# A fused attention and token-MLP kernel: a replanned order of score groups, first loads on two queues, a half-size weight load, and filler matmuls

**Chip, cores, metric.** One core of one Trainium2 chip. The metric is the time of one execution in device microseconds (us). The profile's span is 1.8 us shorter than the time of the same execution.

## The reference, cut to what matters

```python
q, k, v: (8 batches, 12 heads, 448, 64)
scores = (q @ k.T) / 8 - log(448);  x = sigmoid(scores) @ v      # heads side by side: (8, 448, 768)
wq, wk = x @ w_q, x @ w_k                                        # both (8, 448, 64)
mixed  = ((wq @ wk.T) / 8) @ x
out    = relu(mixed) @ w_out
```

## The kernel before

The work is cut into 24 *pairs* (two batches by two heads), each with seven score groups. A string, PLAN, gives the order of TensorE's groups: `S` scores of one group (then a sigmoid on ScalarE), `P` values, `q`/`k` the transposes of one pair's q or k, `x` transposes of the attention output, `W N U M m O` the MLP. Loads and casts follow in a fixed ORDER. Every load passes one queue; GpSimd (Pool) casts it to bf16; TensorE takes everything in the plan's order.

```python
    p_ld = pool("ld", 3)            # load buffers of each of q, k, v
    p_qk = pool("qk", 8)            # transposed q, k
    def scores(n, i):
        ...                                             # 4 matmuls 64x64, k stationary
        nc.scalar.activation(at, sc[:, :, 0:S], ACTF.Sigmoid, bias=bias_t, scale=attn_scale)
    def load_weights():             # w_q and w_k, each for both halves of the partitions
        for b2 in range(2):
            for x, w in enumerate((moe_w_q, moe_w_k)):
                o = 64 * (x ^ b2)
                nc.sync.dma_start(out=wqk32[HALF[b2], :, o : o + 64], in_=w.rearrange("(h d) n -> d h n", d=HD))
    def pump_loads():               # the next load in ORDER, if its buffer's last owner has been cast
        ...
                if n >= 3 and (nm, n - 3) not in cast:
                    break
    def pump():                     # the next cast in ORDER, on Pool
        ...
                    nc.gpsimd.tensor_copy(out=wqk16, in_=wqk32)     # the weights, in their turn
        ...
                cast1(n, nm, nc.gpsimd)
    nc.sync.dma_start(out=q0, in_=src["q"])
    nc.sync.dma_start(out=k0[:, :, cols(KA)], in_=src["k"][:, :, cols(KA)])
    nc.sync.dma_start(out=k0[:, :, cols(KB)], in_=src["k"][:, :, cols(KB)])
    ...                             # cut: 32 matmuls on zeros, then
    tr_part("q", q016, IA, "v")
    tr_part("q", q016, IB, "s")
    tr_part("k", k016, KA, "v", free2[-1])
```

## Time and profile before

| | before |
|---|---|
| time, median of the first 4 runs | 210.30 us (210.11 to 210.66) |
| span of the profiled execution | 209.4 us (this execution took 211.18) |
| first sigmoid | 6.47 us |
| 64th sigmoid (first of pair 9) | 68.33 us |
| from there to the last output chunk | 135.64 us |

The two times at the bottom are starts of single instructions in the trace.

### The profile page before, as it was taken

To read this page: it belongs to the slowest core of one execution; us is meant where nothing else is said; L and a number is where in the kernel's file an instruction comes from. 1 tells how busy PE (TensorE), PEld (TensorE's weight loads), DVE (VectorE), ACT (ScalarE), POOL (GpSimd) and SP (SyncE) were. 2 spreads that over 40 slices of the span, in tenths; PEclk is the share of its full clock that TensorE was granted. 3 is DMA by queue.
4 is the path that set the end of the run, shared out by engine and by line. 5 is a ranking of instruction groups with operands and counts; after the bars stand their busy time and mean duration, and the time that the engine had idled before them with its cause. 6 is when DMAs were issued, how large, how long until landed. Compare 5 with 4: busy or idle time off the path is not lost.

```text
span 209.4 us, 6320 instructions
## 1 busy us (share of the span) xinstructions
PE 197.0 (94%) x2630; PEld 117.5 (56%) x2630; DVE 121.9 (58%) x208; ACT 170.8 (82%) x193; POOL 72.6 (35%) x85
## 2 busy tenths in 40 slices
PE   8498988889999999999999999999999999999991
PEld 7254544556546656656656565655565555655561
DVE  2135555755598746664889675645788654554321
ACT  3689999979999999999998989889898998055220
POOL 2477755577877842730022700251110000000000
PEclk9759999999999999999999999999999999999999
DMA  5999999999999999997065463355203252154785
GB/s 174 374 381 380 381 173 290 381 384 384 383 384 383 379 381 385 399 389 253 5 199 130 145 181 79 78 147 195 51 29 78 75 152 70 27 134 104 200 203 174
DMA packets 28684, 47.59 MB, mean 227 GB/s; under 512 B 5360, under 2 KB 24432, under 8 KB 28656
## 3 DMA queue, kind: packets, MB, share of 16 engines
q1 hardware_dynamic: 27616, 45.03, 67.1%
q10 hardware_dynamic: 1040, 2.16, 2.7%
q8 instruction: 20, 0.33, 0.7%
q14 instruction: 8, 0.07, 0.1%
HBM read 36.18 MB, written 11.01 MB: 225 GB/s over the span
## 4 chain that ended last, share of the span: by engine, by line
PE 75%; DMA 16%; POOL 2%; SPq 1%; ACT 1%; issue 1%; DVE 1%; DVEq 0%; ACTq 0%; POOLq 0%
PE po L283 27%; PE sc L154 15%; PE pv L173 13%; DMA v<-in_v_dram 9%; DMA k<-in_k_dram 8%; PE px L191 5%; PE pw L215 3%; PE ptq L131 3%; PE ptk L131 3%; PE pt L240 3%; PE pm L264 2%; ACT at L159 1%; POOL k L118 1%; POOL v L118 1%; SPq L107 1%; PE pk L227 1%
## 5 line engine op out<-in xcount | busy, mean ns | idle before, releaser
L159 ACT ACTIVATE at<-sc,bias_t 128x896 bf16<-128x896 f32 x168 | 155.4, 1020 | 12.6 <-PE sc L154 11.7
L283 PE MATMUL po<-wout,mx 128*128 128x384 bf16 (+1 forms) x342 | 60.6, 324 | 0.0
L154 PE MATMUL sc<-qt,kt 64*64 64x448 bf16 x672 | 57.7, 367 | 2.5 <-ACT at L159 1.8
L283 PEld LDWEIGHTS <-mx 128*128 128x128 bf16 x342 | 30.9, 98 | 24.3 <-issue 7.0
L173 PE MATMUL pv<-at,v 64*64 64x448 bf16 x672 | 41.8, 352 | 1.1 <-POOL v L118 1.1
L178 DVE CAST xt<-pv 128x896 bf16<-128x896 f32 x24 | 26.2, 1091 | 23.4 <-PE pv L173 23.4
L308 DVE COPY o<-po 128x384 f32<-128x384 f32 x45 | 25.1, 557 | 24.7 <-PE po L283 24.4
L154 PEld LDWEIGHTS <-kt 64*64 64x64 bf16 x672 | 21.9, 105 | 23.7 <-issue 12.6
L118 POOL CAST q<-q 128x896 bf16<-128x896 f32 x23 | 21.5, 933 | 33.3 <-issue 26.3
L118 POOL CAST v<-v 128x896 bf16<-128x896 f32 x24 | 22.3, 934 | 22.6 <-PE pv L173 18.0
L118 POOL CAST k<-k 128x896 bf16<-128x896 f32 x23 | 21.5, 933 | 19.4 <-PE ptk L131 15.7
L173 PEld LDWEIGHTS <-v 64*64 64x64 bf16 x672 | 20.5, 107 | 11.2 <-POOL v L118 1.4
L138 DVE COPY kt<-ptk 128x896 bf16<-128x896 bf16 x23 | 14.3, 620 | 10.3 <-PE ptk L131 10.2
L196 DVE COPY xn<-px 128x512 bf16<-128x512 bf16 x48 | 18.0, 417 | 2.9 <-PE px L191 2.9
L306 ACT COPY o<-po 128x384 f32<-128x384 f32 x10 | 4.8, 478 | 15.7 <-PE po L283 15.7
L256 DVE TENSOR_SCALAR mx<-pm 128x896 bf16<-128x896 f32 x15 | 16.3, 1088 | 1.8 <-PE pm L264 1.4
L138 DVE COPY qt<-ptq 128x896 bf16<-128x896 bf16 x23 | 14.1, 619 | 4.5 <-PE ptq L131 3.7
L131 PE MATMUL ptq<-ident,q 128*128 128x128 bf16 x161 | 13.7, 228 | 1.4 <-POOL q L118 1.4
L191 PE MATMUL px<-ident,xt 128*128 128x128 bf16 x192 | 14.7, 220 | 0.2 <-DVE o L308 0.2
L191 PEld LDWEIGHTS <-xt 128*128 128x128 bf16 x192 | 11.6, 98 | 4.6 <-issue 3.8
L131 PE MATMUL ptk<-ident,k 128*128 128x128 bf16 x161 | 13.3, 224 | 0.6 <-POOL k L118 0.6
L131 PEld LDWEIGHTS <-q 128*128 128x128 bf16 x161 | 9.9, 102 | 6.7 <-issue 3.7
(43 smaller groups left out, 93.8 us busy)
## 6 DMA issues: line engine op xcount, KB each, us to landing
q<-in_q_dram SPq DMA_DIRECT2D x24, 448.0 KB, 8.0
v<-in_v_dram SPq DMA_DIRECT2D x24, 448.0 KB, 7.5
k<-in_k_dram SPq DMA_DIRECT2D x23, 448.0 KB, 7.8
out_dram<-o SPq DMA_DIRECT2D x44, 192.0 KB, 3.0
w<-in_moe_w_out_dram SPq DMA_DIRECT2D x6, 384.0 KB, 5.8
out_dram<-o ACTq DMA_DIRECT2D x10, 192.0 KB, 3.2
wqk<-in_moe_w_q_dram SPq DMA_DIRECT2D x2, 192.0 KB, 9.4
wqk<-in_moe_w_k_dram SPq DMA_DIRECT2D x2, 192.0 KB, 8.5
```

The source lines that it names most:

```text
L118: eng.tensor_copy(out=t16.rearrange("p i b d -> p b i d"), in_=ld.pop((nm, n)).rearrange("p b (i d) -> p b i d", i=NI),)
L131: nc.tensor.transpose(ps[:, i].rearrange("p h n -> p (h n)"), t16[:, i].rearrange("p b d -> p (b d)"), ident16,)
L138: nc.vector.tensor_copy(out=t[:, hs], in_=ps[:, :, hs, :].rearrange("p i h n -> p h i n"))
L154: nc.tensor.matmul(sc[HALF[h], b2, 0:S], qk["k", n][HALF[b2], h, i, :], qk["q", n][HALF[b2], h].rearrange("p i n -> p (i n)"), start=True, ...
L159: nc.scalar.activation(at, sc[:, :, 0:S], ACTF.Sigmoid, bias=bias_t, scale=attn_scale)
L173: nc.tensor.matmul(ps[HALF[b2], h, 0:S], ld["v16", n][HALF[h], i, b2, :], ats[n, i][HALF[h], b2, :], start=(i == 0), stop=(i == NI - 1),)
L178: nc.vector.tensor_copy(out=xts[j][:, :, 0:S], in_=ps[:, :, 0:S])
L191: nc.tensor.transpose(ps[:, m, h].rearrange("p b d -> p (b d)"), xts[j][:, h, m * P : (m + 1) * P], ident16,)
L196: nc.vector.tensor_copy(out=xns[u][:, :, b2, 2 * HD * j : 2 * HD * (j + 1)].rearrange("p m (h d) -> p m h d", h=2), in_=ps[:, :, :, b2, :],)
L256: nc.vector.tensor_scalar(dst, ps, moe_scale, 0.0, ALU.mult, ALU.max)
L283: nc.tensor.matmul(ps, mxs[u][c].rearrange("p b s -> p (b s)")[:, m * P : (m + 1) * P], wout16[:, c, w0:w1], start=(c == 0), stop=(c == NC ...
L308: nc.vector.tensor_copy(out=o[:, nb * NB : (nb + 1) * NB], in_=ps)
```

## The change

Intent: keep ScalarE from running dry in the first 45 us by a better order, bring the first q and k in sooner, and keep the clock of TensorE up.

```diff
-    p_qk = pool("qk", 8)
+    p_qk = pool("qk", 14)
@@ weights: half the bytes, other half copied on chip
-        for b2 in range(2):
-            for x, w in enumerate((moe_w_q, moe_w_k)):
-                o = 64 * (x ^ b2)
-                nc.sync.dma_start(
-                    out=wqk32[HALF[b2], :, o : o + 64], in_=w.rearrange("(h d) n -> d h n", d=HD)
-                )
+        for x, w in enumerate((moe_w_q, moe_w_k)):
+            nc.sync.dma_start(
+                out=wqk32[:, :, 64 * x : 64 * x + 64], in_=w.rearrange("(h d) n -> d h n", d=HD)
+            )
+    def cast_weights():
+        nc.gpsimd.tensor_copy(out=wqk16[HALF[0]], in_=wqk32)
+        nc.gpsimd.dma_start(out=wqk16[HALF[1]], in_=wqk16[HALF[0]])
@@ start
-    nc.sync.dma_start(out=q0, in_=src["q"])
-    nc.sync.dma_start(out=k0[:, :, cols(KA)], in_=src["k"][:, :, cols(KA)])
-    nc.sync.dma_start(out=k0[:, :, cols(KB)], in_=src["k"][:, :, cols(KB)])
+    for t32, nm in ((q0, "q"), (k0, "k")):
+        for b2, eng in ((0, nc.sync), (1, nc.scalar)):
+            eng.dma_start(out=t32[:, b2], in_=src[nm][:, b2])
...
-    for _ in range(32):
-        nc.tensor.matmul(ps[:, 0, 0:P], zeros, zeros, start=True, stop=True)
+    keep_warm(28)
...
     tr_part("q", q016, IB, "s")
+    keep_warm(9)
     tr_part("k", k016, KA, "v", free2[-1])
+    keep_warm(5)
@@ ORDER is now made from the plan: a load stands where its first use stands; weights 6 places before W
+    places = [(first["W"] - 6, 0)] + [(first["O"] - 14 + 2 * c, c) for c in range(1, 7)]
@@ PLAN, rows of pairs 0 to 6 of 24 (D is a filler of two 64x448 matmuls)
-        "SSSKqSSSSkq",
-        "SPPPPPSkSSPkSPqSS",
-        "SxPqSPPPPSPPSqSPPSkPSPP",
-        "SxPSSPkSSSkPPSkP",
-        "SPPPPSqSqSSqxSxSk",
-        "SSqkPPSPPPPSPqSkSSxPPPP",
-        "SPPPSkqSWWWSWWWWSWWWWSWSx",
+        "SSSKPDDDSkSqSPkSPPD",
+        "SPDDSkSPDDSPqSqSSxq",
+        "SPPkSqSPPPPSkSPqSPSPP",
+        "SPPPSPkSkSSSqSx",
+        "SqxPSPqSPkSPPPSPqSqSPPP",
+        "SPPPPSqSxSkSSkxPPSPPP",
+        "SkPSPkSqSWWWSkWSWWWSWWWW",
... (17 rows cut)
```

`keep_warm(n)` issues n matmuls of 128 columns on zeros. Not shown: in `W` the output half is `x ^ b2`, to fit the copied weights.

More of the change, by code (lines that the diff above doesn't have):

```diff
@@ L84 @@
     wqk16 = singles.tile([P, H, P], BF16, name="wqk16")
-    wqk32 = singles.tile([P, H, P], F32, name="wqk32")
+    wqk32 = singles.tile([NP, H, P], F32, name="wqk32")
     ident = singles.tile([P, P], F32)
@@ L215, in mlp_wqk @@
                 nc.tensor.matmul(
-                    ps[HALF[x], b2, 0:S], wqk16[HALF[b2], h, 64 * x : 64 * x + 64],
+                    ps[HALF[x ^ b2], b2, 0:S], wqk16[HALF[b2], h, 64 * x : 64 * x + 64],
                     xts[h // 2][HALF[b2], h % 2, 0:S], start=(h == 0), stop=(h == H - 1),
@@ L336, in load_wout @@
         nc.sync.dma_start(out=w32[c], in_=moe_w_out[c * P : (c + 1) * P, :])
+    PLAN = (
+        "SSSKPDDDSkSqSPkSPPD",
[5 more added lines that the diff above has]
+        "SkPSPkSqSWWWSkWSWWWSWWWW",
+        "SWkSxSPPPSPNSPPPSUSk",
+        "SMqSqSPPPSPPPPSUSMSx",
+        "SkSMxSqmPPPPSPPPSkSMSqkmPPPP",
+        "SPPPSOSSSkOOSS",
+        "SkOqSPPPPSPPPSOSSSkOx",
+        "SPPPPPSPPSxxSWWSWWWWWWSWWSWWx",
+        "SqSPPPSPPPPSOSSSNOq",
+        "SSUUSPPPPSPPPSOSMSkO",
+        "SMmxxSPPPPSPPPSOSMSOqSM",
+        "SxOSMSOqSSPPPPPPPSOS",
+        "SSqOxSPPPPPSPPSOSPPPSkx",
+        "SPPPWWPWWWSWWWWWWSWSxOSSSNOO",
+        "SSSUUPPSPPPPSPOSMSO",
+        "SMOSMSOSPPPSPPPPSOmMSxx",
+        "SPPPSPPPPSOSMSOxSS",
+        "SOOSPPPPSPPPSOSSSOO",
+        "SPPPPSPPPSOSSSxOxS",
+        "PPPPWWPPPWWWWWWWWWWOONxOUOUMmMOOMmmOOOOOOOOOOOOOOOO",
+    )
     IA, IB = slice(0, 4), slice(4, 7)
@@ L362, with keep_warm @@
     nc.scalar.activation(warm, bias_t, ACTF.Sigmoid, bias=bias_t, scale=1.0)
-    fb, ps = bank2("pwarm")
-    for _ in range(32):
-        nc.tensor.matmul(ps[:, 0, 0:P], zeros, zeros, start=True, stop=True)
-    free2.append(fb)
+    def keep_warm(n):
+        fb, ps = bank([P, 512], F32, "pwarm")
+        for _ in range(n):
+            nc.tensor.matmul(ps[:, 0:P], zeros, zeros, start=True, stop=True)
+        free1.append(fb)
+    keep_warm(28)
     for t in xts + [wqk]:
         nc.vector.memset(t[:, :, S:], 0.0)
-    ORDER = [("q", 1), ("k", 1), ("v", 0)]
-    nq = 2
-    for n in range(1, N):
-        for _ in range(2 if n in (1, 2, 3, 4) else 1):
-            if nq < N:
-                ORDER += [("q", nq), ("k", nq)]
-                nq += 1
-        ORDER.append(("v", n))
-    for n, at_ in ((0, 18), (1, 30), (2, 33), (3, 36), (4, 39), (5, 42), (6, 45)):
-        ORDER.insert(at_, ("w", n))
+    STEPS = "".join(PLAN)
+    ORDER, seen = [], dict(q=1, k=1, P=0)
+    first = {}
+    for t in STEPS:
+        if t in "qkP":
+            if t != "P":
+                ORDER.append((t, seen[t]))
+            elif seen[t] % NI == 0:
+                ORDER.append(("v", seen[t] // NI))
+            seen[t] += 1
+        first.setdefault(t, len(ORDER))
+    places = [(first["W"] - 6, 0)] + [(first["O"] - 14 + 2 * c, c) for c in range(1, 7)]
+    for n, (place, c) in enumerate(places):
+        ORDER.insert(place + n, ("w", c))
     used, loaded, cast = set(), set(), set()
@@ L405, in pump @@
                 else:
-                    nc.gpsimd.tensor_copy(out=wqk16, in_=wqk32)
+                    cast_weights()
             else:
@@ L441 @@
     tr_part("q", q016, IB, "s")
+    keep_warm(9)
     tr_part("k", k016, KA, "v", free2[-1])
+    keep_warm(5)
     used |= {("q", 0), ("k", 0)}
     pump()
-    PLAN = (
-        "SSSKqSSSSkq",
-        "SPPPPPSkSSPkSPqSS",
-        "SxPqSPPPPSPPSqSPPSkPSPP",
-        "SxPSSPkSSSkPPSkP",
-        "SPPPPSqSqSSqxSxSk",
-        "SSqkPPSPPPPSPqSkSSxPPPP",
-        "SPPPSkqSWWWSWWWWSWWWWSWSx",
-        "SNPSPPPPSPPSUSqSMUmSMq",
-        "SkSMxSkSPPPSPPPPSqSk",
-        "SMxmqSPPPPSPPPSOSSSOO",
-        "SSkxSSOkSPPPSPPPPSO",
-        "SSSqOkSPPPSPPPPSqxSPPPP",
-        "SPPPSOSSSqOxSWWWWWSWW",
-        "SWWWWWSOSSSNxPPPPPSPPSUU",
-        "SMSxkSPPPPSPPPSOSMSkO",
-        "SMmOkSMSOqSMSqOSPPPPSPPP",
-        "SOSSSkOxSPPPSPPPPSxO",
-        "SSSOOSSxOSPPSPPPPPPPPP",
-        "SPPPSxqSWSWWWWWWSWWWSWWOS",
-        "SSONSSOxSPPPPPPSPSUU",
-        "SSMxOSSPPPPPPPSOSMSkx",
-        "SPPPSPPPPmOSMmqOSMSOqSS",
-        "SkOxSPPPPSPPPSOSSSOOx",
-        "SPSPPPPPPSOSSSOOxS",
-        "WPPPWPPPPWWWWWWWWWWOONxOUUMmmOOmMmOOOOOOOOOOOOOOOO",
-    )
-    done = dict.fromkeys("SPqkKxWNUMO", 0)
+    done = dict.fromkeys("SPqkKxWNUMOD", 0)
     done["q"] = done["k"] = 1
-    for t in "".join(PLAN).replace(" ", ""):
+    for t in STEPS:
         kind = "M" if t == "m" else t
@@ L496 @@
             pump()
+        elif t == "D":
+            fb, ps = bank([P, 512], F32, "pwarm")
+            for x in range(2):
+                nc.tensor.matmul(
+                    ps[HALF[x], 0:S], zeros[HALF[0], 0:64], qk["q", 0][HALF[0], x].rearrange("p i n -> p (i n)"),
+                    start=True, stop=True,
+                )
+            free1.append(fb)
         elif t == "K":
```

## The prediction

> **What bounds the kernel now.** I began with the page: is one engine the bound throughout?
>
> ```profile
> PE 197.0 (94%) x2630; PEld 117.5 (56%) x2630; DVE 121.9 (58%) x208; ACT 170.8 (82%) x193; POOL 72.6 (35%) x85
> ...
> PEclk9759999999999999999999999999999999999999
> ...
> L159 ACT ACTIVATE at<-sc,bias_t 128x896 bf16<-128x896 f32 x168 | 155.4, 1020 | 12.6 <-PE sc L154 11.7
> ```
>
> TensorE (PE) is busy 94% of the span, but ScalarE (ACT) has 168 sigmoids, 155.4 us of work, and stands idle 12.6 us between them. Such shares mix stages, so I cut the span where the picture changes. The columns are the stretch, its length, then the busy time of each engine, the granted clock, the DMA share and GB/s:
>
> ```profile
> 6.00:9.50 3.50, 1.30 (x16) 0.54 (x16) 0.42 (x1) 2.80 (x3) 1.55 (x2) 0.80 1.03 387
> 9.50:14.50 5.00, 4.59 (x41) 2.93 (x45) 1.41 (x3) 3.46 (x4) 3.73 (x4) 0.50 1.06 382
> 14.50:40.50 26.00, 23.54 (x356) 13.18 (x349) 15.32 (x26) 25.59 (x30) 16.23 (x17) 0.99 1.06 321
> 40.50:45.00 4.50, 3.31 (x57) 2.11 (x57) 1.51 (x3) 3.25 (x5) 3.49 (x4) 1.00 1.06 381
> 45.00:68.30 23.30, 23.13 (x371) 13.59 (x369) 17.25 (x28) 23.09 (x26) 18.46 (x22) 1.00 1.05 384
> 68.30:177.70 109.40, 109.40 (x1523) 65.09 (x1524) 72.03 (x118) 101.09 (x110) 27.96 (x31) 1.00 0.56 180
> 177.70:204.00 26.30, 26.09 (x232) 15.27 (x222) 11.03 (x17) 8.68 (x15) 0.00 (x0) 1.00 0.53 135
> ```
>
> I call the 24 groups of seven score tiles "pairs", as the kernel does. Up to about 40 us ACT is the pace: 25.59 of 26.00 us busy, while PE has holes. From 68.3 us, where the scores of pair 9 reach ACT, to 177.7 us PE has no hole at all, and ACT is short of work by 8.3 us. From 177.7 us only PE work is left. So the end is set by: when pair 9 is reached, plus PE's work from there. DMA is full until 68 us.
>
> Second view: which holes are on that path? The timeline of ACT at the beginning:
>
> ```profile
> 6.47 2.80 ACT L159 ACTIVATE at<-sc,bias_t 128x896 bf16<-128x896 f32 x3 [0.76 <-PE sc L154]
> 11.04 3.70 ACT L159 ACTIVATE at<-sc,bias_t 128x896 bf16<-128x896 f32 x4 [1.77 <-PE sc L154]
> ...
> 16.16 26.25 ACT L159 ACTIVATE at<-sc,bias_t 128x896 bf16<-128x896 f32 x29 [0.25 <-PE sc L154]
> 43.66 6.54 ACT L159 ACTIVATE at<-sc,bias_t 128x896 bf16<-128x896 f32 x7 [1.25 <-PE sc L154]
> ```
>
> ACT stops twice, at 9.3 and at 42.4 us, both times for scores that PE has not made. PE itself stood there for loads: from its timeline,
>
> ```profile
> 8.02 0.54 PE L432 MATMUL ptk<-ident,k 128*128 128x128 bf16 x4 [1.22 <-POOL k L421]
> 9.54 0.93 PE L131 MATMUL ptq<-ident,q 128*128 128x128 bf16 x7 [0.99 <-POOL q L118]
> ...
> 41.67 0.56 PE L131 MATMUL ptk<-ident,k 128*128 128x128 bf16 x7 [0.63 <-POOL k L118]
> 42.79 0.57 PE L173 MATMUL pv<-at,v 64*64 64x448 bf16 x8 [0.55 <-POOL v L118]
> ```
>
> PE takes matmuls in order, so a transpose that waits for a late cast holds up the scores behind it.
>
> **What the skill says.** The Trainium skill, "TensorE: Matmul & The Clock Gate", Part 1, says that the array runs at half clock until about 3.4 us of sustained work and again after an idle window of that order. The trace agrees: after the hole from 6.8 us the granted clock is 0.50 in 9.5 to 14.5 us, and seven transposes take 0.93 us there, 0.56 us later. "DMA: Bandwidth & Descriptors", section "Issuing engines are not separate DMA queues", says that loads from several issuing engines share the same 16 engines and that a second issuer saves only issue time. The trace can show the size of that: one issue takes 0.44 us. The same page's table asks for at least 512 B a run at line rate; the weight loads of w_q and w_k are runs of 256 B, and the mean rate in 14.5 to 40.5 us, where they fall, is 321 GB/s against 381 beside it. "TensorEngine Tiling (Array Packing)", Key Properties, says that a change of tiling mode drains TensorE. Agreed: a score tile (four 64x64 matmuls) takes 0.19 us on PE when another 64x64 group follows, 0.29 to 0.31 when a transpose or an output chunk follows; seven transposes 0.40 and 0.49.
>
> **The change, part by part.**
>
> *PE work.* Prices from the distance of one group's start to the next in the PE timeline: S, P, W, M, D groups (scores, values, token weights, mix, filler) 0.19 us; seven transposes 0.40; eight 0.445; output chunk 0.975; a U half 0.67; plus 0.10 for each change of tiling mode. Summed over the old order to the last output chunk: 183.8 us. From pair 9 on the sum is 135.1, and the trace has 67.6 to 204.0, which is 136.4: the prices hold to 1%. The new order has the same groups, plus eight D groups (8 x 0.19 = 1.5 us) and 170 mode changes for 156 (1.4 us): 186.7 us. But 51.4 us of it lie before pair 9, where the old order has 48.7. From pair 9 on it is 135.3 us: +0.2. The extra work lies where PE had holes, and costs nothing unless it delays a score.
>
> *The beginning.* q landed at 4.08 us, the first part of k at 4.63, the second at 7.29; the first scores were at 6.03. Now q and k go in halves by batch, each half on one of two queues, so both parts of k need all of it: 917 KB where 655 KB were enough. At the 381 GB/s seen next that is 0.7 us more, less what issuing in parallel (0.44 us) saves, and less what full 1,792 B rows save over 768 B and 1,024 B ones. I take the first sigmoid at 6.6 us, +0.1. What is gained is the second part of k: about 5.3 us for 7.29. Its transposes no longer hold PE until 8.0.
>
> *The first stall.* After the first three scores the old order has K, then q, whose cast is ready at 9.5. The new one loads v first, then k, q, and puts P and three fillers before the next scores. Counting 1.2 us a load (the pace of landings in the trace), v is there at about 6.4, k of pair 1 at 7.6, q at 8.8, k of pair 2 at 10.0; each with 0.93 us of cast is ready 0.8 to 1.5 us before ACT would run dry at 0.9 us a sigmoid. So ACT should not stop, and the clock should stay up.
>
> *The second stall.* The weight loads are half the bytes (two issues for four; the other half is copied on chip by a DMA that Pool issues) and fall later. I put each further load at 1.2 us, 2.6 us for the two weight loads, and compared with the place of its use: all are in time, closest by about 0.5 us (v of pair 5). So 42.4 us should have no stop.
>
> *The sum.* From 6.47 to 68.30 ACT is idle 3.6 us (61.83 less the 58.19 us of the rows above). One relu eviction of 0.92 us, which ACT did before pair 9, comes after it in the new order. Sigmoids without pauses follow each other by 0.90 us ((26.25 - 1.02)/28), so 63 need 56.7 us, and pair 9 could be at 6.6 + 56.7 = 63.3 us, 5.0 us earlier. I do not give it all of that: PE's work to pair 9 is 51.4 us for 56.7 of ACT, and rows of the new order need 5.9 to 6.7 us of PE for 6.3 of ACT, with only two or three score buffers between. In the old order the 15 pairs after pair 9, tightly coupled too, lost 1.3 us against the prices (136.4 less 135.1). I allow 1.0. Gain 4.0, less the 0.2 of PE: 3.8 us. From 210.38 that is 206.6.
>
> **Rivals.** (a) *PE was the limit already and the early holes are hidden anyway*: then the 2.9 us of more PE work show and the time is 211 to 213. Against it: PE's holes before 45 us are not made up later, as the row from 68.3 has no slack. (b) *The loads still set the pace*: DMA runs at 381 GB/s to 68 us in both, and a misplaced load holds PE. If the first q and k come 1 us later through sharing with v's load on the other queue, or two loads miss by 1 us, the gain halves: 208.5. For it: margins of 0.5 to 1 us. Against: fewer weight bytes and an order made from the order of use. (c) *Coupling costs nothing, the clock stays full and the start is earlier*: 5.0 us plus up to 0.7 of smoothing later, 204.7. (d) *The wider qk pool (14 for 8) alone does the work*: not before 40 us, as no cast there waits for it; it only allows the new order.
>
> **Range and chances.** (c) is the low end and a little more of (b) the high end: 204.5 to 209.0. 2% is at 206.2, just below the middle of what I expect, so faster and same are nearly even: 0.43 and 0.55. Slower by 2% needs a fault such as a second stall of 8 us: 0.02.
>
> **What would show it.** Right, if: the fourth sigmoid follows the third without pause; the clock holds at 1.0 from 5 us; no pause of over 1 us up to 45 us; pair 9 at about 64.3 us on ACT; from there to the last output chunk about 136.5 us, PE without holes; tail after the last sigmoid about 1 us longer than the 31.7 of before, as 1.2 us more of PE's work lies there. Wrong, if the first sigmoid is later than 7.3, if PE waits for casts after 15 us, or if PE shows holes after pair 9.

## The result, and the profile after

213.06 us median of 4 runs (212.13 to 213.6), against 210.30 before: a ratio of 1.0125, 95% interval 1.0086 to 1.0163. It is slower, though by less than 2%. Ratios are the mean time of one kernel's runs over that of the other's of the same rounds, so not quite the ratio of the medians that I quote. Executions over 1.5% slower than the fastest of the same kernel are left out of the means.

The same stretches as in the prediction, for the changed kernel (stretch, length, busy time of PE, PEld, DVE, ACT and POOL, granted clock, DMA share, GB/s):

```profile
6.00:9.50 3.50, 3.50 (x37) 2.21 (x36) 0.36 (x1) 1.28 (x3) 2.27 (x3) 1.00 1.03 383
9.50:14.50 5.00, 5.00 (x74) 3.00 (x74) 2.30 (x4) 5.00 (x6) 3.75 (x4) 1.00 1.05 378
14.50:40.50 26.00, 25.23 (x382) 14.68 (x379) 15.97 (x27) 26.00 (x30) 17.57 (x19) 1.00 1.06 339
40.50:45.00 4.50, 2.19 (x29) 1.52 (x29) 2.12 (x4) 2.93 (x4) 3.66 (x4) 0.86 0.95 311
45.00:68.30 23.30, 23.30 (x343) 13.41 (x341) 13.91 (x22) 20.39 (x23) 16.86 (x20) 0.88 1.02 369
68.30:177.70 109.40, 109.25 (x1516) 63.13 (x1519) 74.34 (x121) 102.07 (x111) 27.94 (x31) 1.00 0.56 176
```

The clock of 1.00 in the first row is not a measurement: the first clock record of this execution is at 9.6 us, and the durations up to there point to half clock (the first twelve score matmuls took 1.33 us from 7.64, and 0.76 in before). From 9.5 to 40.5 us ScalarE (the fourth busy time) is full: 31.00 of 31.00 us, where before it had 29.05. That part of the plan works. Then both TensorE (the first) and ScalarE have a hole, and the clock is below 1. Its timeline says where:

```profile
8.28 35.15 ACT L159 ACTIVATE at<-sc,bias_t 128x896 bf16<-128x896 f32 x39 [2.22 <-PE sc L154]
46.01 1.91 ACT L159 ACTIVATE at<-sc,bias_t 128x896 bf16<-128x896 f32 x2 [2.58 <-PE sc L154]
49.36 1.01 ACT L159 ACTIVATE at<-sc,bias_t 128x896 bf16<-128x896 f32 x1 [1.44 <-PE sc L154]
50.83 10.19 ACT L159 ACTIVATE at<-sc,bias_t 128x896 bf16<-128x896 f32 x11 [0.46 <-PE sc L154]
```

39 sigmoids run without a pause, but from 8.28 us for 6.47; then come pauses of 2.58, 1.44 and 0.46 us. TensorE and Pool, from their timelines around the first pause:

```profile
41.76 0.38 PE L154 MATMUL sc<-qt,kt 64*64 64x448 bf16 x4
44.45 0.93 PE L131 MATMUL ptk<-ident,k 128*128 128x128 bf16 x7 [2.31 <-POOL k L118]
45.31 0.96 PE L154 MATMUL sc<-qt,kt 64*64 64x448 bf16 x8
```

```profile
37.86 0.94 POOL L118 CAST q<-q 128x896 bf16<-128x896 f32 x1 [1.16 <-PE sc L154]
41.04 1.46 POOL L333 CAST wqk<-wqk 64x1536 bf16<-64x1536 f32 x1 [2.24 <-DMA wqk<-in_moe_w_k_dram]
42.80 0.65 POOL L334 DMA_DIRECT2D wqk<-wqk  x1 [0.30 <-POOL wqk L333]
43.45 1.81 POOL L118 CAST k<-k 128x896 bf16<-128x896 f32 x2
```

TensorE stands 2.31 us for the cast of k of pair 9. Pool first waited 2.24 us for the weights, then cast them and issued their copy, and only at 43.45 came to k, which had landed at 41.92. The seven transposes then take 0.93 us for 0.56: the clock is at half. The row of a narrower cut shows for how long (columns as before; the clock is the third number from the end):

```profile
44.00:50.50 6.50, 6.05 (x58) 3.47 (x58) 2.00 (x4) 2.91 (x3) 4.95 (x6) 0.50 0.94 298
```

The 64th sigmoid starts at 69.88 us for 68.33. From it to the last output chunk it is 135.87 us for 135.64, and from there to the end 5.5 for 5.4. So most of what was lost (1.55 of the 1.9 us between the two spans) was lost before pair 9.

### The profile page after: what moved, and what is told of

Same layout as the page of the kernel before. It is cut to its first block, busy times and chain, and to the rows that moved or that the text cites. A ratio compares the mean times of both kernels' runs of the same rounds, so it can differ in the third digit from the quotient of the medians.

```text
span 211.3 us, 6335 instructions
## 1 busy us (share of the span) xinstructions
PE 201.9 (96%) x2656; PEld 118.9 (56%) x2656; DVE 124.2 (59%) x210; ACT 169.0 (80%) x191; POOL 73.4 (35%) x86
## 4 chain that ended last, share of the span: by engine, by line
PE 84%; DMA 9%; POOL 2%; DVE 1%; issue 1%; SPq 1%; ACT 0%; DVEq 0%; ACTq 0%; POOLq 0%
PE po L283 27%; PE sc L154 17%; PE pv L173 13%; PE px L191 5%; DMA q<-in_q_dram 5%; PE ptk L131 5%; PE pw L215 4%; DMA wqk<-in_moe_w_k_dram 4%; PE ptq L131 4%; PE pt L240 3%; PE pm L264 3%; POOL q L118 1%; PE pwarm L514 1%; PE pk L227 1%; PE pwarm L401 1%; POOL wqk L333 1%
## 5 line engine op out<-in xcount | busy, mean ns | idle before, releaser
L154 PE MATMUL sc<-qt,kt 64*64 64x448 bf16 x672 | 59.5, 370 | 0.4 <-ACT at L159 0.3
L173 PE MATMUL pv<-at,v 64*64 64x448 bf16 x672 | 44.0, 357 | 0.4 <-ACT at L159 0.4
L154 PEld LDWEIGHTS <-kt 64*64 64x64 bf16 x672 | 22.7, 106 | 21.2 <-issue 10.4
L256 DVE TENSOR_SCALAR mx<-pm 128x896 bf16<-128x896 f32 x17 | 18.4, 1089 | 1.9 <-PE pm L264 1.8
L131 PEld LDWEIGHTS <-k 128*128 128x128 bf16 x161 | 9.6, 101 | 9.4 <-issue 4.5
L131 PE MATMUL ptq<-ident,q 128*128 128x128 bf16 x161 | 12.9, 220 | 0.0
```

What stands on the lines that cost most here:

```text
L131: nc.tensor.transpose(ps[:, i].rearrange("p h n -> p (h n)"), t16[:, i].rearrange("p b d -> p (b d)"), ident16,)
L154: nc.tensor.matmul(sc[HALF[h], b2, 0:S], qk["k", n][HALF[b2], h, i, :], qk["q", n][HALF[b2], h].rearrange("p i n -> p (i n)"), start=True, ...
L173: nc.tensor.matmul(ps[HALF[b2], h, 0:S], ld["v16", n][HALF[h], i, b2, :], ats[n, i][HALF[h], b2, :], start=(i == 0), stop=(i == NI - 1),)
L256: nc.vector.tensor_scalar(dst, ps, moe_scale, 0.0, ALU.mult, ALU.max)
```

## The experiments

Theory A: the loads set the pace of the first 45 us, and the weights, which stand in the load order in front of k of pair 9, make the stall; the later start is absorbed by it. Theory B: the later start is carried to the end. Theory C: the number of loads alone is too much, wherever the weights lie. Theory D: TensorE's additional work (fillers, mode changes) is what counts. In each run the ratio is to the kernel before, in the same rounds; the changed kernel has 1.0125. Times of single sigmoids are of the one profiled execution, which can be the fastest or the slowest of its four runs.

### First look: start, fillers, weights

**x1_nofill**

```diff
-    keep_warm(9)
...
-    keep_warm(5)
```

> The changed kernel without the 9 and the 5 filler matmuls between the first transposes. The filler stood between the cast of k (done about 5.85) and its transposes (6.65), so the first sigmoid should start at 7.3 to 7.6 us for 8.28. What the end makes of it tells two theories apart. Theory A (loads set the pace until k of pair 9): that load lands at 41.9 whatever the start does, so the pause at the 39th sigmoid gets longer and the end moves by less than 0.4 us. Rival B (late start is carried to the end): 0.7 to 1.0 us faster, 0.4% or more.

212.55 us, ratio 1.0123 (1.0065 to 1.018): no change. The first sigmoid came at 7.21 us, but the 64th later than with fillers, at 71.22. This speaks against B, but the interval is too wide to exclude the 0.4% that B forecast; a3_oldstart below settles it. The profiled execution was the slowest of the four (214.45 us): in it part of the gain was lost at once, since without the fillers the clock fell to half at 9 us and sigmoids 3 to 7 had pauses; the pause behind the 39th was there again.

**x2_w0early**

```diff
-    places = [(first["W"] - 6, 0)] + ...
+    places = [(14, 0)] + ...
```

> The changed kernel with the two loads of w_q and w_k, and their cast, moved from place 25 of the load order to place 14, where each later load has about 2 us of slack. Theory A (the weight loads and their cast lie in front of k of pair 9): k of pair 9 is cast as it lands, near 42 us, without the 1.5 us behind the cast of the weights, and the long pause after the 39th sigmoid goes from 2.6 us to under 1, with one or two pauses of about 1 us earlier instead; 1.5 to 3 us faster. Rival C (the number of loads alone is too much, wherever the weights lie): the same time within 0.7 us. Rival D (the pauses are hidden behind PE work anyway): no change.

213.03 us, ratio 1.0107 (1.0055 to 1.0159): hardly better by the median, rival C's size and not mine. One of the four runs was slow (215.87); the profiled one was the fastest (211.27), with its 64th sigmoid at 67.93 us for 69.88, so in this one execution the move did help. The trace shows what remains. Pool and TensorE, from 24 us:

```profile
24.28 0.94 POOL L118 CAST v<-v 128x896 bf16<-128x896 f32 x1 [0.77 <-DMA v<-in_v_dram]
26.73 1.46 POOL L333 CAST wqk<-wqk 64x1536 bf16<-64x1536 f32 x1 [1.51 <-DMA wqk<-in_moe_w_k_dram]
28.50 0.65 POOL L334 DMA_DIRECT2D wqk<-wqk  x1 [0.30 <-POOL wqk L333]
29.15 1.81 POOL L118 CAST k<-k 128x896 bf16<-128x896 f32 x2
```

```profile
30.15 0.56 PE L131 MATMUL ptk<-ident,k 128*128 128x128 bf16 x7 [2.56 <-POOL k L118]
```

The same picture 14 us earlier: the load behind the weights (here k of pair 6) is late by 2.56 us. The 39th sigmoid now has no pause. The stall goes with the weights.

**x3_noweights** (wrong result)

```diff
-            nc.sync.dma_start(out=wqk32[...], in_=w.rearrange(...))
+            pass
-        nc.gpsimd.tensor_copy(out=wqk16[HALF[0]], in_=wqk32)
-        nc.gpsimd.dma_start(out=wqk16[HALF[1]], in_=wqk16[HALF[0]])
+        pass
+    nc.gpsimd.memset(wqk16, 0.02)          # once, at the start
```

> Wrong result on purpose: w_q and w_k are not loaded or cast, a constant stands in their place. This sizes the cost of these loads. Theory A: the pause after the 39th sigmoid disappears, the clock stays up, 4 to 5.5 us faster than the changed kernel, so 207.5 to 209. Rival D (PE's 2.9 us of additional work is what made the kernel slower): 0 to 1 us faster.

209.20 us, ratio 0.9965 (0.9928 to 1.0002). Against the changed kernel that is 1.6% of the time of before, 3.4 us, somewhat less than the 4 to 5.5 I expected. D falls. A and C are not told apart, as the bytes go together with the stall. ScalarE, from 23 us:

```profile
23.45 45.09 ACT L159 ACTIVATE at<-sc,bias_t 128x896 bf16<-128x896 f32 x50 [0.36 <-PE sc L154]
```

50 sigmoids without a pause; the 64th at 65.73 us. But note the other half of this result: even with its weights for nothing, the new order beats the old kernel by only 0.35%, and the interval includes none.

**x6_noD** (all `D` taken out of PLAN)

> The changed kernel without its eight D fillers (1.5 us of PE by price). I expect no change within 0.5 us, as they lie where ACT is the pace; if PE's additional work is what counts (rival D), 1.5 us faster; if they keep the clock up, the clock drops to half between 9 and 16 us and scores come late there.

212.84 us, ratio 1.0131 (1.0089 to 1.0172): no change, as expected. The clock did not fall before 40 us without them in the profiled execution, so there they were not needed.

### Which part of the change does what

**a3_oldstart**: the changed kernel with the start of before (the diff of the start above, reversed, without the 9 and 5 fillers).

> The changed kernel with the old start: q whole, k in two parts, one queue, 32 fillers, none between the transposes. First sigmoid near 6.5 us. Theory A (load pace decides until the 39th sigmoid): the third load lands about 1.3 us later than in the changed kernel, k of pair 9 too, and the end is 0 to 1.3 us later. Rival B (the late start is carried to the end): 1 to 1.8 us faster.

213.10 us, ratio 1.0171 (1.0106 to 1.0236): the first sigmoid at 6.57 us, 1.7 us earlier than in the changed kernel's profile, and the end no earlier. The 39th sigmoid is followed by a pause of 2.79 us (2.58 in the changed kernel); k of pair 9 landed at 42.83 us for 41.92. B's 1 to 1.8 us would be a ratio of at most 1.008, below the interval. This is the clearest evidence for A against B.

**b1_newstart**: the kernel before with only the new start.

> The kernel before with only the new start: q and k in halves on two queues, 28 + 9 + 5 fillers, old order. First sigmoid 1.0 to 1.8 us later than 6.47, the pause after the third shorter by 1 us or more as q of pair 1 lands a load earlier. Theory: the two cancel, total within 0.7 us of before. If the late start is what counts, 1 to 1.8 us slower.

210.93 us, ratio 1.0037 (0.9999 to 1.0075): 0.6 us slower by the medians and 0.8 by the ratio, so at the edge of the forecast. The way to it was not the expected one: q of pair 1 landed at 8.78 us, no earlier than in before (8.50), and the pause after the third sigmoid shrank from 1.77 to 0.70 us mostly because the first came 0.8 us later (7.25).

**b2_halfw**: the kernel before with only the new weight load.

> The kernel before with only the new weight load: two loads for four, half-size cast, copy on chip by a DMA from Pool. Loads behind it should land 2 to 2.6 us earlier, so the 1.4 us pause at 42 us goes: 0.5 to 1.3 us faster than before. If the copy's wait or Pool's issue costs as much: no change.

210.78 us, ratio 1.0031 (0.998 to 1.0081). A miss: I expected 0.5 to 1.3 us of gain. In the profile the pause at 42 us has gone, but one of 1.56 us stands after the third sigmoid (1.77 in before) and a new one of 0.76 after the 19th, and the start was 0.4 us later. The 64th sigmoid came 0.66 us earlier (67.67); the time after the last chunk's start then took 0.7 us more (see c1 below).

**b12_noorder**: both together in the old order.

> The kernel before with the new start and the new weight load together, in the old order. Each alone was 0.4 and 0.5 us slower in the median, within noise. Expected: within 0.8 us of before. The rest of the difference to the changed kernel (2.7 us less this) is then the order's.

210.94 us, ratio 1.0024 (0.9964 to 1.0084): all of the change but the order (and the wider qk pool that it needs) is neutral within the noise. So the slowdown, about 1% or 2 us, comes with the order, in which the weights' place is included. Its profile started late (first sigmoid 8.23 us) and had hardly a pause after that:

```profile
8.23 24.35 ACT L159 ACTIVATE at<-sc,bias_t 128x896 bf16<-128x896 f32 x27 [2.23 <-PE sc L154]
32.85 11.93 ACT L159 ACTIVATE at<-sc,bias_t 128x896 bf16<-128x896 f32 x13 [0.27 <-PE sc L154]
45.10 3.72 ACT L159 ACTIVATE at<-sc,bias_t 128x896 bf16<-128x896 f32 x4 [0.32 <-PE sc L154]
49.03 9.98 ACT L159 ACTIVATE at<-sc,bias_t 128x896 bf16<-128x896 f32 x11 [0.22 <-PE sc L154]
```

The 64th came at 67.01 us, 58.8 us after the first. In x3_noweights, the new order's best case, these 63 take 58.5 us. So in this execution the old order, with the same weights, did as well before pair 9 as the new one without any. It has the same delay behind the weights: q of pair 8 landed at 34.16 us and was cast only at 35.70, when Pool was through with cast and issue. But TensorE did not need it yet. What differs in the new order is not the delay but the time at which the load behind it is used.

**c1_b12_nofill**: the same without the fillers of the start, 36 ahead of the transposes.

> Old order, new loads of the start, new weight load, no filler between the first transposes, 36 fillers ahead of them for 28. First sigmoid at 6.8 to 7.3 us, 64th at 65.7 to 67 us. If the start is carried to the end in this order (it has few late loads): 0.5 to 1.2 us faster than before, about 209.5. If the loads' pace absorbs it, as in the changed kernel: within 0.5 us of before.

210.84 us, ratio 1.0009 (0.9962 to 1.0056, 5 rounds): equal to before. First sigmoid 7.06, 64th 67.38 us, 0.95 us earlier than in before; but from the start of the last output chunk to the end this execution took 6.41 us for 5.40. The same holds for b1 (5.86), b2 (6.12) and b12 (6.38): what they had won at the 64th sigmoid was largely lost behind the last chunk. I have no run that settles why, so these totals do not show that an earlier pair 9 is worth nothing.

### What the stall is made of

**r1_castdve**

```diff
-        nc.gpsimd.tensor_copy(out=wqk16[HALF[0]], in_=wqk32)
-        nc.gpsimd.dma_start(out=wqk16[HALF[1]], in_=wqk16[HALF[0]])
+        nc.vector.tensor_copy(out=wqk16[HALF[0]], in_=wqk32)      # called behind the x group of score group 38
+        nc.sync.dma_start(out=wqk16[HALF[1]], in_=wqk16[HALF[0]])
```

> The changed kernel, weight loads at the same place, but their cast is done by VectorE (after the eviction behind score group 38) and the copy is issued on the load queue, so that Pool casts k of pair 9 the moment it has landed. It sizes Pool's part of the stall. If the 1.5 to 2.4 us of weight cast and DMA issue on Pool matter: k of pair 9 cast at 42 for 43.5 us, the long pause near 2 us for 3.6, less time at half clock: 1.5 to 2.5 us faster than the changed kernel (about 211). If only the bandwidth that the weight loads take matters: under 0.5 us.

212.04 us, ratio 1.0082 (1.0004 to 1.016): 0.4% better than the changed kernel, less than expected and not clear of the noise. TensorE's timeline, however, is plain:

```profile
42.51 0.56 PE L131 MATMUL ptk<-ident,k 128*128 128x128 bf16 x7 [0.88 <-POOL k L118]
...
44.11 0.56 PE L131 MATMUL ptk<-ident,k 128*128 128x128 bf16 x7 [0.53 <-POOL k L118]
...
50.52 0.75 PE L215 MATMUL pw<-xt,wqk 64*64 64x448 bf16 x10 [0.74 <-DMA wqk<-wqk]
```

The wait of 2.31 us is 0.88 now, the clock stays up, but smaller waits come behind it: for k of pair 10 and for the copy of the weights. With Pool out of the way, the loads are still late (k of pair 9 landed at 41.46 us and was cast at 41.52). The profiled execution was the fastest of the four.

**r4_fill**

```diff
-        "SPPPPSqSxSkSSkxPPSPPP",
+        "SPPPPSqSxSDDDDDDDDDDDDkSSkxPPSPPP",
```

> The changed kernel with twelve more D fillers (2.3 us) in front of the transposes of k of pair 9, where TensorE stood for 2.3 us and the clock then went to half for 6.8 us. It sizes the clock's part of the stall. If the half clock costs what its trace suggests (seven matmul groups at double time, 2 us): the clock stays at 1.0, 1 to 2 us faster than the changed kernel. If loads set the pace after the pause as well: no change.

211.78 us, ratio 1.0065 (1.0004 to 1.0127), 0.6% better; intervals overlap. The row of the same stretch as above:

```profile
44.00:50.50 6.50, 6.23 (x95) 3.51 (x92) 3.46 (x6) 4.63 (x5) 5.26 (x6) 1.00 0.90 279
```

The clock is 1.00 for 0.50, and TensorE does 95 matmuls there (7 of them fillers) for 58. By the medians r4 is 1.3 us faster; that is my estimate of the clock's part of the stall, not shown beyond the noise.

**r2_later3**: cast as in r1, weights three places later in the load order, copy on ScalarE's queue.

> As the run with the cast on VectorE, and the weight loads three places later in the load order, behind k of pairs 9 and 10 and v of pair 5; the copy is issued from ACT's queue. Loads then come in the order in which they are needed. Expected: no pause over 2.5 us, 64th sigmoid at 66 to 67.5 us, 209.5 to 210.5 us, about equal to the kernel before. If the stall only moves to the next load behind the weights as in two runs before (k of pair 11) or to the first use of the weights: 211 to 213.

212.47 us, ratio 1.006 (0.9968 to 1.0153): the interval holds both the kernel before and the changed one, so nothing is decided.

### Could another place or order do it

**x4_later**

```diff
-        "SPPPPSqSxSkSSkxPPSPPP",
+        "SPPPPSSxSSSxPPSPPP",
-        "SWkSxSPPPSPNSPPPSUSk",
-        "SMqSqSPPPSPPPPSUSMSx",
+        "SWkSxSPPPSPNSqPPPSUSk",
+        "SMqSqSPPPSkPPPPSkUSMSx",
```

> The changed kernel with five transposes (k of pairs 9 and 10, q of pair 12, and the ones behind them) taken out of the rows before the weights and put back 3 to 20 score groups later; same work, same weights, the load order follows. Theory A' (the new order asks for three more loads by the 39th sigmoid than the bandwidth gives, and the weights lie among them): the long pause at the 39th sigmoid goes, the 64th sigmoid comes at 66 to 67.5 us for 69.9, and the end 2.5 to 4 us earlier: 209 to 210.5. Rival E (the weights' cast and copy on Pool stop the kernel wherever they are): a pause of over 1.5 us stays and less than 1.5 us is gained.

215.70 us, ratio 1.0269 (1.02 to 1.0337): slower, and my mistake. The weights' place is counted in loads, so taking three loads away from in front of `W` moved the weights ahead, in front of q of pair 11. TensorE waited there:

```profile
42.69 0.93 PE L131 MATMUL ptq<-ident,q 128*128 128x128 bf16 x7 [3.59 <-POOL q L118]
```

A third place for the weights, and a third time the load behind them is the late one.

**y1_later_place**: x4 with the weights behind v of pair 5 (`first["W"] - 3`).

> As x4_later (five transposes later), with the weight loads now behind v of pair 5 and in front of k of pair 9, which is used three score groups later than in the changed kernel. If the longer look-ahead is what the loads can't keep up with: no pause over 2 us before the 46th sigmoid, 64th sigmoid at 66 to 67.5 us, 2.5 to 4 us faster than the changed kernel, 209 to 210.5. If the weights stall whatever is behind them: a pause of 2.5 us or more, and 212 or more.

213.06 us, ratio 1.012 (1.0041 to 1.0199). The first half of the forecast held: no pause of over 0.3 us up to the 53rd sigmoid. The second did not: after the 59th to 61st stood pauses of 0.5 to 1.3 us, as v of pair 7 and k of pairs 14 and 15 were then cast only as TensorE arrived. The 64th was at 68.86 us. The lateness was moved, not removed. The profiled execution was the slowest of the four (214.10), and here too part of the loss lies at the end: 6.73 us from the last chunk's start for 5.53.

**y4_ld4**: four load buffers for three (and 12 of the qk pool for 14, to make room).

> The changed kernel with four load buffers per tensor for three (and 12 transposed buffers for 14, to make room, which should not matter as no more than 12 are alive). The loader waited for buffers at q of pairs 10 to 12; with one more, k of pair 9 should land 0.8 to 1.5 us earlier: 0.8 to 1.8 us faster than the changed kernel. If bandwidth alone is the limit: under 0.4 us.

213.82 us, ratio 1.0153 (1.0083 to 1.0224): no gain, a miss. k of pair 9 landed at 42.08 us, no earlier than in the changed kernel (41.92): buffers were not what held the loads.

**y5_later_ld4**: y1 and y4 together.

> y1 and y4 together: later transposes, weights behind v of pair 5, four load buffers. Expected 208.5 to 210, at or a little under the kernel before; without any stall the 64th sigmoid comes at about 66 us and the span is that plus 141.4.

212.74 us, ratio 1.0136 (1.004 to 1.0231): a miss. Here TensorE waited 1.29 us at the first `W` for the copy of the weights, and the 64th sigmoid came at 68.00 us for the 66 expected.

No version that I tried is faster than the kernel before.

## Why the prediction was wrong

- **The frame was right.** I said that the end is the time at which pair 9 is reached plus TensorE's work from there, and that the new order adds 0.2 us to the latter. In the profiles that stretch (64th sigmoid to last output chunk) is 135.85 to 135.87 us in the new order (the changed kernel, x1, x2, x3, x4, x6, r1, y4, y5) and 135.62 to 135.64 us in the old (before, b1, b2, b12, c1): +0.24. Three profiles have more: a3 136.06, r4 136.13, y1 136.66. The tail after the last sigmoid grew from 31.7 to 32.8 us, as forecast. What the frame left out is the time after the last chunk's start: 5.4 to 5.7 us in most profiles, but 5.9 to 6.4 in b1, b2, b12 and c1 and 6.7 in y1.
- **"ACT should not stop, and the clock should stay up"** at the first stall: right; ScalarE ran without a pause from the first to the 39th sigmoid.
- **"I take the first sigmoid at 6.6 us"**: 8.28 in this execution, 7.1 to 7.6 in most others with this start. I had not looked at the fillers: nine of them stand in front of the transposes of k, cost 0.9 us at half clock, and end at 6.65, where k's cast was through by about 5.9. All of k landed at 5.29 as I had said (5.3). But this term was not what counted: a3_oldstart takes it away and ends no earlier.
- **"42.4 us should have no stop": this is the step that failed.** Counting as the prediction does, 1.2 us a load from 6.4 and 2.6 for the weights, k of pair 9 lands at 39.0 us. It landed at 41.92. The terms: v of pair 0 landed at 7.18 for 6.4 (0.8); the next 23 loads came at 1.24 us on average (0.9, nearly all of it in two gaps of 1.9 and 1.6 us); and from there q of pair 12, the weights and k took 6.2 us for 5.0 (1.2). The weights' 256-byte packets ran from 35.5 to 39.5 us, so q of pair 12, which landed at 37.71 after a gap of 2.0 us, shared the DMA with them. Pool's cast of the weights and its DMA issue, 2.4 us from 41.04 to 43.45, which held the cast of k until 1.5 us after its landing, I left out, and so the half clock that followed the hole. A margin of "0.5 us at the closest" could carry none of this. From the first to the 64th sigmoid I allowed 57.7 us, and it took 61.6: the three gaps after the 39th, 41st and 42nd cost 4.85 us more than three sigmoids, less the 1.0 I had allowed for coupling.
- **Rival (b)**, "the loads still set the pace", was the right one. I sized it at half the gain; it took all of it and 2.7 us more.
- **The size of the prize was too large as well.** Without any weights (x3) the new order gains 0.35%, not my 1.8%. Part of it is that I took the profiled execution of before for a typical one. It took 211.18 us, against a median of 210.38 then, so about 0.8 of the 5.0 us I meant to win may have been that execution's bad luck (if the difference lay before pair 9, which is not shown). Most of the rest is the start (7.23 us for 6.6) and pauses in pairs 0 to 2.

What stays open: bandwidth, Pool and clock overlap in the stall, and their shares (r1: 0.4%, r4: 0.6%, of 1.6% in all) are each within the noise of the other. Theories A and C differ little in the end: r1, y1 and b12 say that what counts is how close behind a landing the load is used, and no run separates the weights' bytes from their odd shape. Whether some third order, with W later, could use the gain of x3 was not tried. Executions of the new order also seem to scatter more (212 to 214 us; y5: 211.3 to 214.4), and I have no run that settles why; the time at which the clock rises differs between executions, and I hold that for likely, not shown.

## What to carry to other kernels

An order that moves uses forward also moves the deadlines of their loads: before counting the engine time gained, list for each load when it lands and when it is used, with everything that stands in the same queue and on the casting engine between them. A one-time load of odd shape in a stream of regular ones delays whatever is behind it by its transfer and its cast, wherever it is put; whether that stalls the kernel depends on the slack of the load behind it (2.3 us of wait in the changed kernel, none that ScalarE felt beyond 0.3 us in b12), and in some executions the clock fell in the hole. And check whether the profiled execution is a typical one before calling its idle time the prize.

## What the Trainium skill lacked or had wrong

- "TensorE: Matmul & The Clock Gate", Part 1, gives about 4 us of sustained work and half a microsecond of spread until the full clock. With matmuls from 1.0 us on, the first rise in the clock records of these profiles came anywhere from 3.7 us (x2) and 3.9 (x3) to 9.6 (the changed kernel; b12 likewise). A hole of 2.3 us at 42 us was enough for 6.8 us at half clock in the changed kernel, less than the idle window of 3.4 us that the page names; in before one of 1.22 us (6.8 to 8.0) was enough, so that the prediction's "the trace agrees" holds for the half speed and not for the length of the window; and in y4 one of 2.52 us left the clock at 1.00. The profile's clock column shows 1.00 before its first record, also where nine 128-column matmuls took 1.12 us; the durations are to be trusted there.
- "DMA: Bandwidth & Descriptors", section "Why small descriptors are slow (HBM only)", puts 256-byte descriptors at 27% overhead. Here that is near the best half microsecond and not the mean: while the weights' runs of 256 B were on their way, the DMA moved at best 253 GB/s (before, 32.0 to 32.5) and 259 (changed kernel, 36.5 to 37.0), a third less than the 381 beside it, but on average 148 (before, 27.0 to 32.5) and 226 (changed kernel, 35.5 to 39.5), larger packets included.
- The same page's section "Issuing engines are not separate DMA queues" says that a second issuer saves only issue time. q landed at 4.11 us for 4.08 with two queues, which agrees; and beyond that nothing is shown: the third 448 KB of loads landed at 7.18 us for 8.50 in the two profiles compared, but with the same start at 8.55 in x4 and 8.78 in b1, and with the old start at 7.58 in a3.
- No page that I found has the time of a copy within SBUF issued by Pool behind a full load queue: 196 KB took 4.3 us from issue to landing in the changed kernel, 6.0 in x2_w0early, and 3.1 (y1) to 7.4 (b12) in all runs that issue it from Pool.
